# Gated linear attention, spectral mixing and a gated MLP on one core: the attention state kept compact, y in two PSUM banks, and a new order of the work

## The chip, the cores and the metric

The program runs on one NeuronCore of a Trainium2 chip. The metric is the device time of one launch in microseconds. Times of whole runs are medians over a few launches; everything about single instructions comes from one profiled execution of the kernel before. PE is TensorE (its weight loads are PEld), DVE VectorE, ACT ScalarE, POOL GpSimd, SP the engine that issues the transfers.

## The reference, cut

Three stages follow each other, on batch 4, sequence 768, 8 heads of 48 columns (384 channels):

```python
# 1. attention: a state of 48 x 48 for each head, decayed by alpha for each row
for t in range(S):
    state = alpha[:, :, t, :, None] * state + einsum('bhd,bhe->bhde', k[:, :, t], v[:, :, t])
    y[:, :, t] = einsum('bhd,bhde->bhe', q[:, :, t], state)
x = y as (batch, seq, 384)
# 2. spectral mixing
theta = x @ w_theta
zr, zi = x * cos(theta), x * sin(theta)
u = x + w_tok_r @ zr + w_tok_i @ zi          # 768 x 768 over the tokens
x = u + relu(u @ w_ch)
# 3. gated MLP
h = relu(x @ w_in)                           # 384 -> 1024
out = (h * sigmoid(conv3(h, conv_w))) @ w_out
```

Tokens are cut into 24 chunks of 128 (6 for each batch). Inside a chunk the attention is a product of scores with v; from chunk to chunk the state carries the rest.

## The kernel before

**Attention, per chunk.** VectorE runs two scans over alpha (L346, L360) and multiplies q and k by them (L375). TensorE makes the transposed k, `kps` (L395), and the scores `sc` (L398 to L405): eight products whose contraction is the 48 rows of one head; the even heads of the pairs lie on partitions 0 to 47, the odd ones on 64 to 111, and the two kinds go to two PSUM tiles in turn. ScalarE copies the scores out (`pt`, L410), GpSimd cuts the causal triangle (L411). Then `a_y` (L425) writes `y`, one PSUM tile of 128 x 384: 32 products `y<-v_t,pt` of 48 columns, each for 32 output rows, and, from a batch's second chunk on, 16 products `y<-S,qk_t`. For these the state S is 128 x 4 x 96: a pair of heads is a block of 96 columns, of which each head uses its own 48, the others are zero. `a_kv` (L448) makes the chunk's addition to the state: for chunks 0 to 11 (`FINEK`) in 8 products of 64 rows and 96 columns, after that in 16 products of 32 rows and 48 columns. `a_state` (L461) adds it to S (one sum of 112 x 384 at L477, or, from chunk 12 on, two of 48 x 192 at L475; a plain copy L472 in a batch's first chunk) and multiplies by the chunk's decay on GpSimd (L479, two instructions). ScalarE copies y to `x` (L446), TensorE transposes it (`xps`, L492), ScalarE copies that to `u` (L497).

**Mixing.** `th` is x @ w_theta, then `zf` goes ScalarE, VectorE, ScalarE (two sines), VectorE (L546, then L561) and is split in a high and a low part (L570 on ScalarE, `zl` L582 on VectorE). `m_mix` (L591) adds one chunk's share to `yps`: for three column blocks d and real and imaginary part, three products (high by high, high by low, low by high), so 18 for a half of the output tokens. For the chunks in `PLAINS` of batch 0 (0 and 1) z is kept in one piece, `zh<-x,zf`, and each of the 6 products is a full fp32 one, with w_tok in one piece too. `m_out_of` (L615) adds `yps` to u, once for each batch and half; for batch 2's second half that is called the sum (2,1) below. Weights arrive in 64-bit words that VectorE decodes in three steps (L169 to L171) before the split (L122 on ScalarE, L123 on VectorE).

**What sets the order.** The attention and `th` of batches 0 to 2, the mix of batches 0 and 1 and the scores of chunk 18 follow `ORDER`, a written list of steps; `in_order` (L652) holds each engine's instructions to that order. After it, the rest of batch 3's attention (chunks 18 to 23), the mix of batches 2 and 3, the decoding of w_ch, w_in and w_out and the MLP are placed by the framework's scheduler. Five PSUM banks (`ps_a`) are shared by y, kv, sc, kps, xps and th, three by yps. In this kernel the four quarters of w_in are loaded and decoded while batch 2's second half is mixed, through one staging buffer that is free when the attention's buffers are closed.

Of the kernel before, what the change touches and what calls it, by code (L numbers as in the profile page):

```python
# [43 lines left out]
PLAINS = (0, 1)  # L44
BYDMA = ()
ZBYDMA = ()
FINEY = 0
FINEK = 2 * NC
EARLY = 99
ORDER = (  # L50
# [44 lines left out]
def tile_gated_linear_attention__then__spectral_moe__then__conv_gate(  # L95
# [53 lines left out]
    def body(top, slow):  # L149
# [919 lines left out]
```

## Time and profile before

| what | us |
|---|---|
| median of 3 runs (lowest, highest) | 556.52 (554.0, 557.42) |
| the profiled execution | 554.66 |
| its span on the core | 552.9 |
| PE busy | 539.0 (97%) |
| DVE busy | 445.3 (81%) |
| ACT busy | 327.7 (59%) |
| POOL busy | 141.2 (26%) |

The profiled execution has 1.8 us around its span. TensorE's granted clock is 1.0 throughout. A matmul's duration in the rows includes its way through the array and overlaps the next one; what it costs in a stream is the distance from its start to the next start. An fp32 product stands as two records in the trace, an fp32r one as one.

### The profile page before, as it was taken

How to read it: one execution, taken by the hardware profiler on the slowest of the kernel's cores; microseconds unless marked ns; L12 is line 12 of the kernel's file. 1: busy time of each engine (PE TensorE's matmuls, PEld its weight loads, DVE VectorE, ACT ScalarE, POOL GpSimd, SP SyncE). 2: the span in 40 equal slices, each digit the busy share in tenths (PEclk: the TensorE clock that was granted, in tenths of full speed). 3: DMA queues.
4: the chain of work that ended last, by engine and by line, in shares of the span. 5: the costliest groups of instructions: out<-in, count | busy, mean ns of one | idle time of the engine just before them, and what ended most of it. 6: DMA issues, size and time to landing. Idle time of an engine off the chain costs nothing.

```text
span 552.9 us, 13205 instructions
## 1 busy us (share of the span) xinstructions
PE 539.0 (97%) x5421; PEld 473.9 (86%) x5423; DVE 445.3 (81%) x697; ACT 327.7 (59%) x699; POOL 141.2 (26%) x195
## 2 busy tenths in 40 slices
PE   7889999999999999999999999999999999999996
PEld 4567788688999999989998988898998898999896
DVE  7999999988975876753978789998989969969520
ACT  3657865656647683553743238757678567558621
POOL 2557644602122303450000002122224002314000
PEclk9999999999999999999999999999999999999999
DMA  8663664761132231401143351043253651500011
GB/s 327 190 236 102 227 204 133 241 191 48 30 116 79 88 112 36 134 29 58 59 140 116 117 187 42 0 145 127 86 188 129 219 181 55 205 28 16 30 45 47
DMA packets 24997, 65.56 MB, mean 119 GB/s; under 512 B 2529, under 2 KB 8673, under 8 KB 24545
## 3 DMA queue, kind: packets, MB, share of 16 engines
q1 hardware_dynamic: 24928, 64.64, 35.7%
q8 instruction: 44, 0.72, 0.5%
q14 instruction: 25, 0.20, 0.1%
HBM read 59.92 MB, written 4.72 MB: 117 GB/s over the span
## 4 chain that ended last, share of the span: by engine, by line
PE 85%; DVE 6%; DMA 5%; POOL 1%; issue 1%; ACT 0%; DVEq 0%; ACTq 0%; SPq 0%; POOLq 0%
PE yps L114 23%; PE ops L114 18%; PE hps L114 18%; PE cps L114 7%; PE th L114 6%; PE y L114 5%; PE sc L114 4%; DMA stage<-in_w_in_dram 3%; PE kv L114 2%; PE xps L492 1%; PE kps L395 1%; DVE fbt L346 1%; DMA stage<-in_w_tok_dram 1%; POOL S L479 1%; DVE stage L170 1%
## 5 line engine op out<-in xcount | busy, mean ns | idle before, releaser
L114 PE MATMUL yps<-wtok,zh 128*128 128x384 f32 x528 | 139.0, 343 | 1.1 <-DVE u L618 1.1
L114 PE MATMUL ops<-wout,g 128*128 128x384 f32 x576 | 104.4, 336 | 0.0
L114 PE MATMUL hps<-us,win 128*128 128x512 f32 x432 | 103.5, 390 | 0.0
L114 PEld LDWEIGHTS ops<-wout,g 128*128 128x128 f32 x576 | 101.0, 188 | 1.7
L114 PEld LDWEIGHTS yps<-wtok,zh 128*128 128x128 f32 x528 | 93.8, 188 | 4.7 <-DVE u L618 1.4
L114 PEld LDWEIGHTS hps<-us,win 128*128 128x128 f32 x432 | 80.8, 188 | 15.7
L114 PE MATMUL yps<-wtok,zl 128*128 128x384 f32 x264 | 87.4, 335 | 0.0
L842 DVE SCALAR_TENSOR_TENSOR cv<-hh,cw,cv 128x510 f32<-128x510 f32 (+7 forms) x128 | 74.7, 617 | 5.0 <-ACT cv L835 4.7
L411 POOL TENSOR_SCALAR_AFFINE_SELECT pt<-pt 128x512 f32<-128x512 f32 x48 | 51.5, 1087 | 99.1 <-ACT pt L410 95.5
L114 PEld LDWEIGHTS yps<-wtok,zl 128*128 128x128 f32 x264 | 49.5, 188 | 0.1
L123 DVE TENSOR_TENSOR g<-cv,g 128x384 fp32r<-128x384 f32 (+2 forms) x96 | 37.1, 423 | 10.3 <-ACT g L122 10.2
L479 POOL TENSOR_TENSOR S<-tst,ftot 48x192 f32<-48x192 f32 x32 | 34.2, 1068 | 39.1 <-DVE tst L475 19.0
L825 ACT ACTIVATE hh<-hps 128x512 f32<-128x512 f32 x48 | 28.5, 595 | 21.6 <-PE hps L114 12.5
L114 PE MATMUL cps<-us,wch 128*128 128x512 f32 x162 | 40.2, 390 | 0.0
L346 DVE TENSOR_TENSOR_SCAN fbt<-a_t,onehot 128x516 f32<-128x516 f32 x24 | 31.4, 1307 | 10.9 <-ACT a_t L367 9.1
L122 ACT CAST g<-cv 128x1 fp32r<-128x1 f32 (+3 forms) x128 | 37.2, 350 | 4.6 <-DVE cv L860 4.0
L860 DVE SCALAR_TENSOR_TENSOR cv<-cv,hh 128x511 f32<-128x511 f32 (+2 forms) x48 | 32.6, 691 | 7.1 <-ACT cv L859 7.1
L883 ACT ACTIVATE ob<-ops 128x384 f32<-128x384 f32 x24 | 11.7, 490 | 42.1 <-PE ops L114 42.1
L114 PEld LDWEIGHTS cps<-us,wch 128*128 128x128 f32 x162 | 30.4, 188 | 6.0
L835 ACT ACTIVATE cv<-hh,cw 128x511 f32<-128x511 f32 (+2 forms) x48 | 34.4, 724 | 1.4 <-POOL hh L828 0.7
L410 ACT COPY pt<-sc 128x512 f32<-128x512 f32 x48 | 26.7, 588 | 14.2 <-PE sc L114 10.2
L832 POOL COPY edge<-hh 128x2 f32<-128x2 f32 x32 | 14.3, 451 | 81.1 <-ACT hh L825 70.0
(101 smaller groups left out, 880.5 us busy)
## 6 DMA issues: line engine op xcount, KB each, us to landing
qk_t<-in_qka_dram SPq DMA_DIRECT2D x24, 512.0 KB, 4.9
stage<-in_w_tok_dram SPq DMA_DIRECT2D x12, 768.0 KB, 4.9
top<-in_w_tok_dram SPq DMA_DIRECT2D x12, 768.0 KB, 4.5
a_t<-in_qka_dram SPq DMA_DIRECT2D x24, 260.0 KB, 3.0
v_t<-in_v_dram SPq DMA_DIRECT2D x24, 192.0 KB, 4.1
out_dram<-ob SPq DMA_DIRECT2D x24, 192.0 KB, 1.9
stage<-in_w_in_dram SPq DMA_DIRECT2D x4, 768.0 KB, 4.4
stage<-in_w_out_dram SPq DMA_DIRECT2D x4, 768.0 KB, 4.4
```

The costliest lines, as they stand in the source:

```text
L114: nc.tensor.matmul(o, lhsT, rhs, start=start, stop=stop, skip_group_check=True)
L122: cast = nc.scalar.copy(hi, src)
L123: lo_eng.tensor_tensor(lo, src, hi.bitcast(F32), ALU.subtract)
L346: nc.vector.tensor_tensor_scan(bf[:, AW:0:-1], at[:, AW:0:-1], of[:, AW:0:-1], 0.0, ALU.mult, ALU.add)
L410: marks["pt"] = nc.scalar.copy(pt, scs[j])
L411: nc.gpsimd.affine_select(pt, pt, [[0, NP], [1, P]], ALU.is_ge, 0.0, base=0, channel_multiplier=-1)
L479: nc.gpsimd.tensor_tensor(Sn[r, :, e], tt[r, :, e], nft[r].unsqueeze(2).to_broadcast([D, NP, D]), ALU.mult)
L825: nc.scalar.activation(hh[:, 2:], ps, AF.Relu)
L832: nc.gpsimd.tensor_copy(edges[n][:, f], hh[:, CH : CH + 2])
L835: nc.scalar.activation(cv[:, a:e], hh[:, a + 1 : e + 1], AF.Copy, scale=cw[:, f, 1:2])
L842: nc.vector.scalar_tensor_tensor(cv[:, lo:hi], hh[:, lo + k : hi + k], cw[:, f, k : k + 1], cv[:, lo:hi], ALU.mult, ALU.add)
L860: nc.vector.scalar_tensor_tensor(cv[:, a:e], cv[:, a:e], 1.0, hhs.pop((n, f))[:, a + 1 : e + 1], ALU.add, ALU.mult)
```

## The change

The state S becomes 128 x 4 x 48: each head's own columns only. Its product `y<-S,qk_t` contracts over the 48 partitions of one head and writes 64 rows and 48 columns. The two heads of a pair lie on different partitions, so y is now two PSUM tiles, one for the even heads, one for the odd ones, each half of a bank wide; the first one's other half holds the chunk's addition `kv`, always in products of 32 rows and 48 columns. x is copied out in two instructions. The state's sum and its decay are one instruction each in every chunk, on 112 partitions x 192. `PLAINS` gets a third chunk. The loads of w_in move behind those of w_ch, after the scheduled loop, and the first decode step of each load that is issued there is ordered behind the sum (2,1). `ORDER` is a new list. The list's `warm` products, which only keep TensorE running at the start, are 36 in place of 39.

```diff
-PLAINS = (0, 1)
+PLAINS = (0, 1, 2)
...
-    "... kt.0 pt0.0 pt1.0 sq.1 tot.1 warm.9 y.0 kv.0 st.0 mul.1 "
+    "... fore.1 pt0.0 tot.1 pt1.0 kt.0 sq.1 mul.1 warm.9 kps.1 sc.1 y.0 kv.0 "
...
-            Sst = [acon.tile([P, NP, 2 * D], F32, name=f"S{i}") for i in range(2)]
+            Sst = [acon.tile([P, NP, D], F32, name=f"S{i}") for i in range(2)]
...
-                y = ps_a.tile([P, DM], F32, tag="a", name="y")
+                ybs = [ps_a.tile([P, 2, NP, D], F32, tag="a", name="y") for _ in range(2)]
+                y = [yb[:, 0] for yb in ybs]
+                if c < NC - 1:
+                    kvs[ci] = ybs[0][:, 1]
...
-                        for t in parts:
-                            mm(y[t, p * 96 : p * 96 + 96], qh[:, p, t], Sp[:, p, :], False, True)
+                        for t in (slice(0, 64), slice(64, P)):
+                            for j in range(2):
+                                r = slice(64 * j, 64 * j + D)
+                                mm(y[j][t, p], qh[r, p, t], Sp[r, p, :], False, True)
...
-                marks["x"] = nc.scalar.copy(xs[ci], ys.pop(ci))
+                xv = xs[ci].rearrange("p (a j d) -> p a j d", a=NP, j=2)
+                for j, yj in enumerate(ys.pop(ci)):
+                    marks["x"] = nc.scalar.copy(xv[:, :, j], yj)
...
-                        for i in range(0, P, rows):
-                            o = 2 * p * D + (i // 64 * D if fine else 0)
-                            mm(kv[i : i + rows, p, :], kt[:, p, i : i + rows], vt[:, o : o + wide], p == 0, True)
+                        for i in range(0, P, 32):
+                            o = 2 * p * D + i // 64 * D
+                            mm(kvs[ci][i : i + 32, p], kt[:, p, i : i + 32], vt[:, o : o + D], False, True)
...
-                        for r, e in own:
-                            nc.scalar.copy(Sn[r, :, e], kv[r, :, slice(0, D) if fine else e])
-                    elif fine:
-                        for r, e in own:
-                            nc.vector.tensor_tensor(tt[r, :, e], Sp[r, :, e], kv[r], ALU.add)
+                        nc.scalar.copy(Sn[:112], kv[:112])
                     else:
                         nc.vector.tensor_tensor(tt[:112], Sp[:112], kv[:112], ALU.add)
-                    for r, e in own:
-                        nc.gpsimd.tensor_tensor(
-                            Sn[r, :, e], tt[r, :, e], nft[r].unsqueeze(2).to_broadcast([D, NP, D]), ALU.mult
-                        )
+                    nc.gpsimd.tensor_tensor(
+                        Sn[:112], tt[:112], nft[:112].unsqueeze(2).to_broadcast([112, NP, D]), ALU.mult
+                    )
...
+            for k, ins in enumerate(decoding(full, st, n)):
+                if k == 0 and not slow:
+                    behind(ins, ("sum",))
...
+            marks["sum"] = sums[B - 2, 1]
...
+            for i in range(len(WIN_EARLY), 4):
+                load_in(i)
```

How this moves instructions, at three places. Names: `y<-S_113` and `y<-S_114` are the state's products (two buffers in turn), `y<-v_t,kt` after the change is the product that was `kv<-v_t,kt`, L114, L395, L492 are L113, L396, L488 afterwards.

TensorE near 36 us, from the `th` of chunks 1 and 2 to the scores of chunk 5, before:

```order
L114 MATMUL th<-whole,u 128x384 x6
L114 MATMUL yps<-full,zh 128x384 x2
L114 MATMUL y<-v_t,pt 32x48 x32
L114 MATMUL y<-S_114,qk_t 32x96 x16
L114 MATMUL kv<-v_t,kt 64x96 x8
L114 MATMUL yps<-full,zh 128x384 x2
L395 MATMUL kps<-ident,qk_t 128x128 x4
L492 MATMUL xps<-ident,x 128x128 x3
L114 MATMUL sc<-qk_t 128x128 x16
```

and after the change, from the `th` of chunk 2 to the scores of chunk 5:

```order
L113 MATMUL th<-whole,u 128x384 x3
L113 MATMUL yps<-full,zh 128x384 x4
L113 MATMUL y<-v_t,pt 32x48 x32
L113 MATMUL y<-S_114,qk_t 64x48 x16
L113 MATMUL y<-v_t,kt 32x48 x16
L396 MATMUL kps<-ident,qk_t 128x128 x4
L113 MATMUL sc<-qk_t 128x128 x8
L488 MATMUL xps<-ident,x 128x128 x3
L113 MATMUL yps<-full,zh 128x384 x4
L113 MATMUL sc<-qk_t 128x128 x8
```

Four units of plain mix (two products of `yps<-full` each) stand ahead of chunk 5's scores where there were two.

TensorE in the scheduled loop, around the scores of chunk 20, before:

```order
L492 MATMUL xps<-ident,x 128x128 x3
L395 MATMUL kps<-ident,qk_t 128x128 x4
L114 MATMUL sc<-qk_t 128x128 x8
L114 MATMUL y<-v_t,pt 32x48 x32
L114 MATMUL y<-S_114,qk_t 32x96 x16
L114 MATMUL kv<-v_t,kt 32x48 x16
```

and after the change, the same chunk:

```order
L113 MATMUL y<-v_t,kt 32x48 x16
L488 MATMUL xps<-ident,x 128x128 x3
L396 MATMUL kps<-ident,qk_t 128x128 x4
L113 MATMUL sc<-qk_t 128x128 x4
L113 MATMUL yps<-wtok,zh 128x384 x2
L113 MATMUL yps<-wtok,zl 128x384
L113 MATMUL yps<-wtok,zh 128x384 x2
L113 MATMUL yps<-wtok,zl 128x384
L113 MATMUL yps<-wtok,zh 128x384 x2
L113 MATMUL yps<-wtok,zl 128x384
L113 MATMUL yps<-wtok,zh 128x384 x2
L113 MATMUL sc<-qk_t 128x128 x4
```

The scores come as four of the even heads, mix products, and four of the odd heads (so for chunks 20, 21 and 22), and the state's addition no longer follows the state's product but stands after 13 to 21 mix products. Of the mix, 216 products (all of batch 2's) stand before batch 3's `th`, where there were 179; all six `th` (54 products) now follow each other.

VectorE behind the attention, before; `win` is the low part of a quarter of w_in, L517 the low part of x for `th`:

```order
L169 TENSOR_SCALAR stage<-stage 128x768
L170 SCALAR_TENSOR_TENSOR stage<-stage 128x768
L517 TENSOR_TENSOR zh<-u,zh 128x384
L171 SCALAR_TENSOR_TENSOR stage<-stage 128x768
L546 SCALAR_TENSOR_TENSOR zf<-zf,th 128x384
L123 TENSOR_TENSOR win_3639<-stage,win_3638 128x3x256
L546 SCALAR_TENSOR_TENSOR zf<-zf,th 128x384
L561 TENSOR_TENSOR zf<-x,zf 128x768 x2
L582 TENSOR_TENSOR zl<-zf,zh 128x768
```

and after the change (L614 is the sum (2,1), L168 to L170 the three decode steps, L513 the low part of x, L542, L557, L578 the three steps to `zl`):

```order
L614 TENSOR_TENSOR u<-yps,u 128x384 x3
L168 TENSOR_SCALAR stage<-stage 128x768
L169 SCALAR_TENSOR_TENSOR stage<-stage 128x768
L513 TENSOR_TENSOR zh<-u,zh 128x384
L170 SCALAR_TENSOR_TENSOR stage<-stage 128x768
L542 SCALAR_TENSOR_TENSOR zf<-zf,th 128x384 x2
L557 TENSOR_TENSOR zf<-x,zf 128x768 x2
L578 TENSOR_TENSOR zl<-zf,zh 128x768 x2
L542 SCALAR_TENSOR_TENSOR zf<-zf,th 128x384
L122 TENSOR_TENSOR wch_3955<-stage,wch_3954 128x768
```

The first weights decoded there are w_ch's, behind the sum (2,1); w_in's four quarters follow later, two of them ahead of the sums of batch 3's first half.

## Rows read from the trace of the kernel before

**Rows 1.** The page: busy time of TensorE.
```profile
PE 539.0 (97%) x5421; PEld 473.9 (86%) x5423; DVE 445.3 (81%) x697; ACT 327.7 (59%) x699; POOL 141.2 (26%) x195
```

**Rows 2.** The page: the chain that ended last, shares by engine.
```profile
PE 85%; DVE 6%; DMA 5%; POOL 1%; issue 1%; ACT 0%; DVEq 0%; ACTq 0%; SPq 0%; POOLq 0%
```

**Rows 3.** Two stretches: busy us of PE, PEld, DVE, ACT, POOL; clock, DMA.
```profile
50.00:100.00 50.00, 49.77 (x794) 39.53 (x786) 48.67 (x58) 35.60 (x74) 26.94 (x21) 1.00 0.60 188
...
350.00:400.00 50.00, 50.00 (x248) 44.67 (x247) 48.02 (x98) 34.28 (x81) 13.29 (x28) 1.00 0.28 93
```

**Rows 4.** TensorE's waits: for whom, us in total, times, longest.
```profile
PE yps L114 <- DVE u L618: 1.1, 1, 1.1
PE kv L114 <- issue: 1.1, 1, 1.1
PE y L114 <- POOL pt L411: 0.7, 2, 0.5
```

**Rows 5.** TensorE in order of time at 93 us (start, us, operation): an early chunk.
```profile
93.85 0.84 PE L114 MATMUL y<-S,qk_t 128*32 128x96 f32 x32
94.62 0.88 PE L114 MATMUL kv<-v_t,kt 128*64 128x96 f32 x16
95.44 0.66 PE L395 MATMUL kps<-ident,qk_t 128*128 128x128 f32 x4
96.02 1.16 PE L114 MATMUL sc<-qk_t 48*128 48x128 f32 x16
97.11 1.24 PE L114 MATMUL yps<-full,zh 128*128 128x384 f32 x3
```

**Rows 6.** The same at 223 us: a late chunk.
```profile
223.99 0.84 PE L114 MATMUL y<-S,qk_t 128*32 128x96 f32 x32
224.65 0.52 PE L114 MATMUL kv<-v_t,kt 128*32 128x48 f32 x32
225.10 0.44 PE L114 MATMUL yps<-wtok,zh 128*128 128x384 f32 x1
225.38 0.34 PE L114 MATMUL yps<-wtok,zl 128*128 128x384 f32 x1
```

**Rows 7.** The same at 100 us: plain mix, up to the next product.
```profile
100.77 2.74 PE L114 MATMUL yps<-full,zh 128*128 128x384 f32 x8
103.45 0.89 PE L114 MATMUL y<-v_t,pt 128*32 128x48 f32 x64
```

**Rows 8.** The chain that ended last, in order of time: start, us, what.
```profile
43.77 1.99 PE sc L114 x32
...
203.65 11.30 PE yps L114 x64
...
252.45 5.25 DMA stage<-in_w_in_dram
...
262.73 4.35 DMA stage<-in_w_in_dram
...
318.51 5.44 PE hps L114 x24
```

**Rows 9.** Groups of instructions by shape: count, busy us, mean ns; idle before.
```profile
L582 DVE TENSOR_TENSOR zl<-zf,zh 128x768 fp32r<-128x768 f32 x22 | 21.3, 972 | 2.6 <-ACT zh L570 2.5
L561 DVE TENSOR_TENSOR zf<-x,zf 128x768 f32<-128x768 f32 x22 | 21.1, 963 | 2.9 <-ACT zf L555 2.9
...
L475 DVE TENSOR_TENSOR tst<-S,kv 48x192 f32<-48x192 f32 x16 | 5.6, 350 | 8.7 <-PE kv L114 8.4
...
L477 DVE TENSOR_TENSOR tst<-S,kv 112x384 f32<-112x384 f32 x8 | 4.3, 541 | 0.6 <-PE kv L114 0.6
```

**Rows 10.** VectorE in order of time: product of chunk 5, then z of chunk 1.
```profile
42.63 1.22 DVE L375 TENSOR_TENSOR qk_t<-qk_t,fbt 128x1024 f32<-128x1024 f32 x1
...
45.82 1.26 DVE L561 TENSOR_TENSOR zh<-x,zf 128x768 f32<-128x768 f32 x1
```

**Rows 11.** GpSimd in order of time: one chunk's decay.
```profile
52.87 4.70 POOL L479 TENSOR_TENSOR S<-tst,ftot 48x192 f32<-48x192 f32 x2 [1.36 <-DVE tst L477]
```

More of the change, by code (lines that the diff above doesn't have):

```diff
@@ L38 @@
 NWARM = 13
+WIN_EARLY = ()
 OB = 2
@@ L43 @@
 WHOLE = 2
-PLAINS = (0, 1)
+PLAINS = (0, 1, 2)
 BYDMA = ()
 ZBYDMA = ()
-FINEY = 0
-FINEK = 2 * NC
 EARLY = 99
 ORDER = (
[36 rows of a table removed]
[36 rows of a table added]
 )
@@ L180, in load_split @@
             full = st[:, 1536 : 1536 + n]
-            decode(full, st, n)
+            for k, ins in enumerate(decoding(full, st, n)):
+                if k == 0 and not slow:
+                    behind(ins, ("sum",))
             if scale is not None:
@@ L429, in a_y @@
                 Sp = Sst[ci % 2]
-                y = ps_a.tile([P, DM], F32, tag="a", name="y")
-                rows = 32 if ci >= FINEY else 64
-                parts = [slice(i, i + rows) for i in range(0, P, rows)]
+                ybs = [ps_a.tile([P, 2, NP, D], F32, tag="a", name="y") for _ in range(2)]
+                y = [yb[:, 0] for yb in ybs]
+                if c < NC - 1:
+                    kvs[ci] = ybs[0][:, 1]
                 for j in range(2):
@@ L435, in a_y @@
                         h = 2 * p + j
-                        for t in parts:
-                            mm(y[t, h * D : (h + 1) * D], pts[j][:, p, t], vt[:, h * D : (h + 1) * D], h == 0, c == 0)
+                        for i in range(0, P, 32):
+                            t = slice(i, i + 32)
+                            mm(y[j][t, p], pts[j][:, p, t], vt[:, h * D : (h + 1) * D], p == 0, c == 0)
                 if c > 0:
                     for p in range(NP):
-                        for t in parts:
-                            mm(y[t, p * 96 : p * 96 + 96], qh[:, p, t], Sp[:, p, :], False, True)
+                        for t in (slice(0, 64), slice(64, P)):
+                            for j in range(2):
+                                r = slice(64 * j, 64 * j + D)
+                                mm(y[j][t, p], qh[r, p, t], Sp[r, p, :], False, True)
                 ys[ci] = y
@@ L451, in a_kv @@
                 if ci % NC < NC - 1:
-                    fine = ci >= FINEK
-                    rows, wide = (32, D) if fine else (64, 2 * D)
-                    kv = ps_a.tile([P, NP, wide], F32, tag="a", name="kv")
                     for p in range(NP):
-                        for i in range(0, P, rows):
-                            o = 2 * p * D + (i // 64 * D if fine else 0)
-                            mm(kv[i : i + rows, p, :], kt[:, p, i : i + rows], vt[:, o : o + wide], p == 0, True)
-                    kvs[ci] = kv
+                        for i in range(0, P, 32):
+                            o = 2 * p * D + i // 64 * D
+                            mm(kvs[ci][i : i + 32, p], kt[:, p, i : i + 32], vt[:, o : o + D], False, True)
             def a_state(ci):
@@ L466, in a_state @@
                     nft = prep[ci + 1][2] if ci + 1 in prep else half[ci + 1][4]
-                    fine = ci >= FINEK
-                    own = [(slice(64 * j, 64 * j + D), slice(j * D, (j + 1) * D)) for j in range(2)]
-                    tt = Sn if c == 0 else att.tile([P, NP, 2 * D], F32, tag="tst", name="tst", bufs=1)
+                    tt = Sn if c == 0 else att.tile([P, NP, D], F32, tag="tst", name="tst", bufs=1)
                     if c == 0:
-                        for r, e in own:
-                            nc.scalar.copy(Sn[r, :, e], kv[r, :, slice(0, D) if fine else e])
-                    elif fine:
-                        for r, e in own:
-                            nc.vector.tensor_tensor(tt[r, :, e], Sp[r, :, e], kv[r], ALU.add)
+                        nc.scalar.copy(Sn[:112], kv[:112])
                     else:
                         nc.vector.tensor_tensor(tt[:112], Sp[:112], kv[:112], ALU.add)
-                    for r, e in own:
-                        nc.gpsimd.tensor_tensor(
-                            Sn[r, :, e], tt[r, :, e], nft[r].unsqueeze(2).to_broadcast([D, NP, D]), ALU.mult
-                        )
+                    nc.gpsimd.tensor_tensor(
+                        Sn[:112], tt[:112], nft[:112].unsqueeze(2).to_broadcast([112, NP, D]), ALU.mult
+                    )
             def a_xt(ci):
@@ L587, in a_theta @@
                     f(ci)
-            mixps = {}
+            mixps, sums = {}, {}
             def m_mix(b, h, c, ds=range(KD)):
@@ L617, in m_out_of @@
                 for d in ds:
-                    nc.vector.tensor_tensor(ub[b][:, d, hs], mixps[d][:, :HALF], ub[b][:, d, hs], ALU.add)
+                    sums[b, h] = nc.vector.tensor_tensor(ub[b][:, d, hs], mixps[d][:, :HALF], ub[b][:, d, hs], ALU.add)
             def a_att(b, c):
@@ L712, in body, with load_in @@
                     win = [win_p.tile([P, KD, DFF], F32R, name=f"win{i}") for i in range(2)]
+                    def load_in(i):
+                        ns = slice(i * 256, (i + 1) * 256)
+                        wi = w_in.rearrange("(k p) f -> p k f", p=P).bitcast(U32)[:, :, 512 * i : 512 * (i + 1)]
+                        load_split(None, "w", wi, [KD, 256], win[0][:, :, ns], win[1][:, :, ns])
                 for c in range(NC):
@@ L715, in body @@
                     a_theta((b + 1) * NC + c)
-                    if b == B - 2 and c < 4:
-                        ns = slice(c * 256, (c + 1) * 256)
-                        wi = w_in.rearrange("(k p) f -> p k f", p=P).bitcast(U32)[:, :, 512 * c : 512 * (c + 1)]
-                        load_split(None, "w", wi, [KD, 256], win[0][:, :, ns], win[1][:, :, ns])
+                    if b == B - 2 and c in WIN_EARLY:
+                        load_in(WIN_EARLY.index(c))
             in_order(first, last)
```

72 rows, old and new, of the table ORDER are left out of this document.

## The prediction

> **What bounds the kernel now.** I read the page first: TensorE is busy for 539.0 of 552.9 us [rows 1], and 85% of the chain that ended last is TensorE's own work [rows 2]. Next its waits: the three that this change can touch come to 2.9 us [rows 4]. So a change pays here by the work that it takes from TensorE or by the order in which that work is fed, and what it spares the other engines pays nothing by itself. Then the stretches: from 50 to 100 us VectorE is busy for 48.67 of 50 us beside a full TensorE, and again for 48.02 from 350 to 400 [rows 3]. There a step of VectorE that comes late has little room to be made good. Last, TensorE in order of time, for what each product costs.
>
> **The change part by part.** The sum is made against the profiled execution, 554.66 us, which lies 1.9 below the median of the runs, 556.52; what comes out is put on the median.
>
> *The state's addition (kv).* By the starts, the old form costs 95.44 - 94.62 = 0.82 us [rows 5], the fine form 225.10 - 224.65 = 0.45 [rows 6]. Ten chunks (0 to 4 and 6 to 10) change from one to the other: -0.37 x 10 = **-3.7**.
>
> *The state's product.* Before, it costs 0.77 us where the old kv follows [rows 5] and 0.66 where the fine one does [rows 6]; what differs is the shape of the tile that comes next, so a change of shape costs about 0.11. The new product has the record count of the fine kv and its 48 columns, spread over two row and two column halves of the array. I take kv's 0.45 plus one change of shape in and some more for the two row halves: 0.65. That is -0.1 in 8 chunks and nothing in the other 12: **-0.8**. Nothing in the trace has this shape; below, it could cost 0.45 (-5.1 in all: 8 x 0.32 + 12 x 0.21); above, if the two row halves don't run side by side, 1.1 (+7.9: 8 x 0.33 + 12 x 0.44). The scores, which also use two row halves, take 1.09 us for 16 records [rows 5], and I take the value near the rows.
>
> The Trainium skill has a rule that speaks against this part: in "TensorEngine Tiling (Array Packing)", section "Key Properties", it says that "Changing tiling mode (not just tile) drains the TensorE". The 0.77 against 0.66 agrees with it. By the rule the new product adds such a drain in each of 20 chunks, and the sum is the one made here; without it, the lower bound of the product would hold.
>
> *A third plain chunk.* Plain mix costs (103.45 - 100.77) / 8 = 0.335 us a record [rows 7], split mix 11.30 / 64 = 0.177 [rows 8]. Chunk 2 of batch 0 has 36 split products, now 12 plain ones of two records: 24 x 0.335 - 36 x 0.177 = **+1.6**. It spares VectorE one `zl` (0.97) and ScalarE one cast.
>
> *The start.* Before, chunk 5's scores are over at 45.8 us [rows 8], with two units of plain mix behind TensorE. After, the order has four units ahead of them, so 2 x 4 x 0.335 = 2.7 us more work. What feeds them is VectorE's product for chunk 5, at 43.85 us [rows 10]. In the new order it stands behind one z more (1.26) and two first decode steps less (about 1.1), and three sums are smaller, 0.35 in place of 0.54 [rows 9]: 43.5. The scores (1.0 for 16 records, half of rows 8's first) then end at 44.7. So TensorE is 45.8 - 44.7 + 2.7 = 3.8 us ahead, of which chunks 0 to 3 had 1.8 by the two parts above: **-1.9**, with 1.5 either way for what I can't follow of ScalarE.
>
> *Smaller state steps.* The decay is one instruction in place of two; near 53 us the pair took 4.70 us [rows 11], and y waited for the triangle behind it, 0.7 in two waits [rows 4]: **-0.5**. The other sums and decays become shorter in the shadow of TensorE, as the mix products cover them. The second copy of x puts some 0.15 us a chunk on ScalarE, which is idle for 40% of the span; if a transpose did wait for each, that would be 3.6.
>
> *The scheduled loop.* Three chunks have their scores split. In one batch of eight, records run two at a time, 1.09 us; in a half nothing runs beside, so eight records take the pairs' time again plus the change of shape, 1.1 us for each half: +1.1 x 3 = **+3.3** (between 0 and 4). The state's addition alone between mix products has its own way in and out, some 0.1 each (225.38 - 225.10 = 0.28 for a first mix product that costs 0.177 in a stream [rows 6, 8]): 5 x 0.2 = **+1.0**.
>
> *Behind the attention.* Here the change adds a wait: VectorE's first decode step is ordered behind the sum (2,1) and waits for w_ch, and behind it in the queue stand the six chunks' `zf` and `zl`, for which batch 3's mix waits. Count from the start of the first transfer, at 252.45 before [rows 8]. It takes 5.25 us. Then VectorE has, up to `zl` of the fifth chunk, 6 `zf` of 0.5, 6 of 0.92 and 5 `zl` of 0.93 by their distances (means 0.963 and 0.972 [rows 9]), 0.5 for x, two decodes of 2.5 and two low parts of 0.95: 20.5. The second transfer (4.35 [rows 8]) starts when the first buffer has been read and has only some 3.3 us of this beside it, so 1.1 is waited, and ScalarE's sines hold VectorE for another 1 or 2: some 28.5 us. TensorE comes to that chunk after 19 mix products, a transpose, 54 `th` and 72 mix products: 145 x 0.175 + 0.3 = 25.7. So it waits for 2.8, and 0.2 at the first chunk: +3.0. The waits before in this stretch, 1.1 for the sum and 1.1 at a kv [rows 4], go: -2.2. Together **+0.8**, between -2 and +5. The last two quarters of w_in are decoded beside the second half's mix, over before the first `hps` (at 318.51 before [rows 8]).
>
> Sum: -3.7 - 0.8 + 1.6 - 1.9 - 0.5 + 3.3 + 1.0 + 0.8 = -0.2. On the median: **556.3 us**. The list gains some 5 us up to chunk 18, and the scheduled part gives them back.
>
> **The rivals.**
>
> *Faster: a change of the array's shape costs nothing beyond the records.* For it: `y<-v_t,pt` has four tiles at a time with no loss; against it: the 0.11 above. Then the state's product is at its lower bound (-4.3 on the sum), kv alone costs nothing (-1.0), and the six half scores lose their 0.2 (-1.2): 556.3 - 6.5 = **549.8**.
>
> *Slower: VectorE runs late into the MLP.* The four decodes of w_in, 3.4 us each, stood before 293 us, where VectorE had idle time. Two of them (6.9) now come later, and what they push, w_out's decodes, reaches the stretch from 350 us, where 2.0 of 50 us are free [rows 3]: 4.9 us that TensorE would wait for taps, and the wait behind the attention at 4 instead of 3. 556.3 + 5.9 = **562.2**. It decides from the point where TensorE's `hps` products stop following each other without a gap. Against it: between the sums of the first half and the first `hps` TensorE has 25 us of its own, and VectorE needs about 20 there.
>
> *Slower: the two row halves of the state's product run one after the other:* +8.7 over my term, **565.0**. The scores speak against it.
>
> **How the numbers follow.** The forecast has 0.64, the first rival 0.17, the second 0.13, the third 0.06. A measurement of this kernel can tell about 1%, 5.6 us, from no change. Faster by more: two thirds of the first rival and the end of the forecast's own spread, 0.17; slower by more: half of the second, the third, and the spread, 0.16; within 1%: 0.67. The range takes in -5.1 of the product's bounds beside the start's -1.5, and on the other side the +5 behind the attention and most of the second rival: 550.0 to 562.0.
>
> **What would show it.** In the profile after: kv at 0.45 us in an early chunk and the state's product at 0.6 to 0.7; chunk 5's scores over near 44.7 us with four plain units behind them; the loop's first 64 mix products beginning near 198.5 instead of 203.65; half scores of 1.1 us in three chunks; TensorE waiting some 3 us in all for `zl` behind the six `th`; and `hps` beginning at about the same time as before. It is wrong if the state's product costs under 0.5 or over 0.9, if `hps` begins more than 4 us away from 318.4, or if TensorE has gaps behind it.

## The result: 1.3% slower

| what | before | after |
|---|---|---|
| median of the runs, us (lowest, highest) | 555.60 (554.0, 557.42) | 562.96 (561.74, 564.21) |
| the profiled execution, its span | 554.66, 552.9 | 563.82, 562.1 |

The kernel before has one more run here than in the table of the start, hence 555.60 for 556.52. The ratio of the runs on record is 1.0126, 95% interval 1.0103 to 1.0150 (the quotient of the two medians is 1.0133). I had forecast 556.3, no change.

The page of the kernel after: busy time, and the chain that ended last by engine.

```profile
PE 544.7 (97%) x5567; PEld 473.1 (84%) x5568; DVE 437.7 (78%) x688; ACT 329.2 (59%) x718; POOL 109.0 (19%) x175
...
PE 90%; DVE 2%; DMA 2%; ACT 1%; issue 1%; ACTq 0%; DVEq 0%; SPq 0%
```

Against [rows 1], GpSimd and VectorE do less (141.2 to 109.0, 445.3 to 437.7), and that pays nothing: TensorE is still nearly all of the chain, 90% for the 85% of [rows 2], and it is busy for 5.7 us more. TensorE's waits after the change (for whom, us in total, times, longest):

```profile
PE xps L488 <- ACT x L453: 3.4, 2, 2.9
...
PE yps L113 <- DVE u L614: 2.2, 1, 2.2
PE yps L113 <- ACT zh L566: 1.2, 1, 1.2
...
PE y L113 <- ACT x L453: 0.8, 1, 0.8
```

The first and the last line are new beside [rows 4]: TensorE waits for x, ScalarE's copy of y. Four points of the program cut the difference to pieces (`hps` are the products with w_in, `cps` those with w_ch, `ops` those with w_out). They are read from TensorE's starts in order of time (some 0.1 us ahead of the chain's of [rows 8]); the forecast is that of the prediction.

| point, us | before | forecast | after | miss in the piece up to it |
|---|---|---|---|---|
| chunk 5's scores are over | 45.7 | 44.7 | 49.8 | +5.1 |
| the scheduled loop's mix begins | 203.6 | 198.5 | 205.8 | +2.2 |
| the first `hps` | 318.4 | 318.4 | 326.5 | +0.8 |
| end of the span | 552.9 | 552.7 | 562.1 | +1.3 |

Of the last +1.3, 1.1 lies behind TensorE's last product: from there to the end of the span it takes 5.8 us after the change and 4.7 before. That tail is between 4.7 and 6.4 us in all the runs below, and no edit aims at it. Most of the miss lies in the first 50 us. TensorE there, in order of time:

```profile
17.96 0.89 PE L113 MATMUL y<-v_t,pt 128*32 128x48 f32 x64
18.78 0.68 PE L113 MATMUL y<-S,qk_t 48*64 48x48 f32 x32
19.39 0.55 PE L113 MATMUL y<-v_t,kt 128*32 128x48 f32 x32
19.87 0.55 PE L488 MATMUL xps<-ident,x 128*128 128x128 f32 x3
23.32 0.55 PE L488 MATMUL xps<-ident,x 128*128 128x128 f32 x3 [2.90 <-ACT x L453]
23.70 0.63 PE L396 MATMUL kps<-ident,qk_t 128*128 128x128 f32 x4
24.26 2.08 PE L113 MATMUL sc<-qk_t 48*128 48x128 f32 x16
26.27 6.45 PE L113 MATMUL th<-whole,u 128*128 128x384 f32 x12
```

y and kv of chunk 1 are over at 19.87, yet its transposes start at 23.32, 2.90 us after TensorE could. ScalarE, which has to copy x for them:

```profile
19.20 0.52 ACT L453 COPY x<-y 128x192 f32<-128x192 f32 x2
22.73 0.54 ACT L453 COPY x<-y 128x192 f32<-128x192 f32 x2 [3.00 <-DVE tst L474]
```

It copies chunk 0's x, then sits idle for 3.00 us until VectorE has made the state's sum `tst` of chunk 1, and VectorE has two scans ahead of that:

```profile
21.21 1.23 DVE L361 TENSOR_TENSOR_SCAN fbt<-a_t,starts 128x516 f32<-128x516 f32 x1
22.36 0.33 DVE L474 TENSOR_TENSOR tst<-S,y 112x192 f32<-112x192 f32 x1
```

x does not need the sum. But kv now lies in the bank of half of y, so x and the sum read one bank, and the program puts the two engines' reads of it one behind the other; in the list, the sum of chunk 1 stands ahead of its x. The groups of x over the whole run, first of the kernel after, then of the one before (busy us, mean ns | idle before, and what ended it):

```profile
L453 ACT COPY x<-y 128x192 f32<-128x192 f32 x48 | 13.2, 328 | 19.4 <-DVE tst L474 11.3 <-PE y L113 8.0
```

```profile
L446 ACT COPY x<-y 128x384 f32<-128x384 f32 x24 | 11.5, 481 | 11.4 <-PE y L114 11.3
```

11.3 us of waiting for VectorE's sum is new. Then TensorE's clock. Three stretches after the change, and the same three before (length, busy us of PE, PEld, DVE, ACT, POOL, granted clock, DMA share, GB/s):

```profile
20.00:24.00 4.00, 1.10 (x9) 0.86 (x10) 3.90 (x7) 1.27 (x5) 0.75 (x1) 1.00 0.95 360
24.00:28.00 4.00, 4.00 (x22) 2.98 (x21) 2.87 (x4) 2.65 (x6) 0.91 (x2) 0.52 1.02 328
28.00:32.00 4.00, 4.00 (x9) 2.09 (x9) 0.87 (x2) 1.34 (x3) 0.31 (x1) 0.63 0.16 59
```

```profile
20.00:24.00 4.00, 2.76 (x42) 2.38 (x40) 3.64 (x7) 1.66 (x5) 0.12 (x1) 1.00 0.32 31
24.00:28.00 4.00, 3.40 (x14) 1.56 (x12) 3.87 (x5) 3.63 (x8) 3.85 (x3) 1.00 0.98 366
28.00:32.00 4.00, 2.69 (x116) 2.41 (x116) 4.00 (x5) 1.15 (x3) 1.70 (x2) 1.00 0.93 313
```

After the change TensorE works for 1.10 of 4 us, and then its granted clock is 0.52: nearly all of that stretch at the lower of its two levels, 1.2 GHz. The 16 score records take 2.01 us there (24.26 to 26.27) in place of 1.09 [rows 5], and twelve `th` 6.38 (26.27 to 32.65).

In the scheduled loop the forecast held. Chunk 20 and the neighbours of its scores:

```profile
223.12 0.55 PE L113 MATMUL y<-v_t,kt 128*32 128x48 f32 x32
...
224.51 1.16 PE L113 MATMUL sc<-qk_t 48*128 48x128 f32 x8
225.60 0.62 PE L113 MATMUL yps<-wtok,zh 128*128 128x384 f32 x2
...
227.73 1.16 PE L113 MATMUL sc<-qk_t 48*128 48x128 f32 x8
228.82 0.89 PE L113 MATMUL y<-v_t,pt 128*32 128x48 f32 x64
229.64 0.68 PE L113 MATMUL y<-S,qk_t 48*64 48x48 f32 x32
230.25 0.44 PE L113 MATMUL yps<-wtok,zl 128*128 128x384 f32 x1
```

Each half of the scores costs 1.09 us, as much as the whole did, and kv stands alone (a lone kv below: mix products on both sides).

### The profile page after: what moved, and what is told of

The parts are those of the page before. It is cut to its first block, busy times and chain, and to the rows that moved or that the text cites. A ratio compares the mean times of both kernels' runs of the same rounds, so it can differ in the third digit from the quotient of the medians.

```text
span 562.1 us, 13445 instructions
## 1 busy us (share of the span) xinstructions
PE 544.7 (97%) x5567; PEld 473.1 (84%) x5568; DVE 437.7 (78%) x688; ACT 329.2 (59%) x718; POOL 109.0 (19%) x175
## 4 chain that ended last, share of the span: by engine, by line
PE 90%; DVE 2%; DMA 2%; ACT 1%; issue 1%; ACTq 0%; DVEq 0%; SPq 0%
PE yps L113 25%; PE ops L113 18%; PE hps L113 17%; PE th L113 8%; PE y L113 7%; PE cps L113 7%; PE sc L113 5%; PE xps L488 2%; PE kps L396 1%; DMA stage<-in_w_in_dram 1%; DMA stage<-in_w_ch_dram 1%; DVE zl L578 0%; DVE stage L169 0%; DVE fbt L347 0%; ACT x L453 0%
## 5 line engine op out<-in xcount | busy, mean ns | idle before, releaser
L113 PE MATMUL yps<-wtok,zh 128*128 128x384 f32 x504 | 130.6, 343 | 3.5 <-DVE u L614 2.2
L113 PE MATMUL ops<-wout,g 128*128 128x384 f32 x576 | 104.1, 336 | 0.0
L113 PE MATMUL hps<-us,win 128*128 128x512 f32 x432 | 103.6, 390 | 0.0
L113 PEld LDWEIGHTS ops<-wout,g 128*128 128x128 f32 x576 | 101.0, 188 | 1.6
L113 PEld LDWEIGHTS yps<-wtok,zh 128*128 128x128 f32 x504 | 89.4, 188 | 7.0 <-DVE u L614 2.5
L113 PEld LDWEIGHTS hps<-us,win 128*128 128x128 f32 x432 | 80.8, 188 | 15.9
L113 PE MATMUL yps<-wtok,zl 128*128 128x384 f32 x252 | 83.0, 337 | 0.0
L845 DVE SCALAR_TENSOR_TENSOR cv<-hh,cw,cv 128x255 f32<-128x255 f32 (+7 forms) x128 | 75.2, 616 | 4.7 <-ACT cv L838 4.4
L412 POOL TENSOR_SCALAR_AFFINE_SELECT pt<-pt 128x512 f32<-128x512 f32 x48 | 41.9, 885 | 122.8 <-ACT pt L411 122.7
L113 PEld LDWEIGHTS yps<-wtok,zl 128*128 128x128 f32 x252 | 47.1, 188 | 0.5 <-DVE zl L578 0.3
L113 PE MATMUL cps<-us,wch 128*128 128x512 f32 x162 | 40.7, 390 | 0.0
L862 ACT ACTIVATE cv<-cv 128x511 f32<-128x511 f32 (+2 forms) x48 | 29.9, 628 | 9.9 <-DVE cv L845 9.6
L113 PEld LDWEIGHTS cps<-us,wch 128*128 128x128 f32 x162 | 30.3, 188 | 5.9
L113 PE MATMUL sc<-qk_t 48*128 48x128 f32 x384 | 32.3, 291 | 0.0
L113 PEld LDWEIGHTS sc<-qk_t 48*128 48x128 f32 x384 | 27.0, 193 | 5.3 <-issue 3.2
```

Source lines behind the costliest of these rows:

```text
L113: nc.tensor.matmul(o, lhsT, rhs, start=start, stop=stop, skip_group_check=True)
L412: nc.gpsimd.affine_select(pt, pt, [[0, NP], [1, P]], ALU.is_ge, 0.0, base=0, channel_multiplier=-1)
L845: nc.vector.scalar_tensor_tensor(cv[:, lo:hi], hh[:, lo + k : hi + k], cw[:, f, k : k + 1], cv[:, lo:hi], ALU.mult, ALU.add)
L862: nc.scalar.activation(cv[:, a:e], cv[:, a:e], AF.Tanh, scale=0.5)
```

## The experiments

My theory from this trace: kv in y's bank (a part to which the prediction gave no price) makes x late; TensorE idles, its clock falls; the rest is what shape changes, lone kv and half scores cost. Rivals: the late loads of w_in; the new list with its third plain chunk; a clock that costs nothing because TensorE would wait anyway. Fifteen runs, each with its ratio to the kernel before and the 95% interval; the points are those of the table above, from one profiled execution each. Those of early and oldorder were the fastest of their four runs, 1.3 and 3.1 us below the median. In early, oldorder and oldkv 16 to 18 more `cps` products, about 4 us, stand ahead of the first `hps`, so that point and the pieces that end there can't be set beside the others' as they are.

| kernel | median us | ratio | chunk 5's scores over | loop's mix | first `hps` | end of span |
|---|---|---|---|---|---|---|
| after | 562.96 | 1.0126 (1.0103 to 1.0150) | 49.8 | 205.8 | 326.5 | 562.1 |
| warm | 560.72 | 1.0088 (1.0055 to 1.0121) | 46.6 | 201.5 | 323.8 | 558.6 |
| x1 | 560.43 | 1.0071 (1.0047 to 1.0096) | 45.0 | 200.5 | 319.8 | 557.3 |
| ownbank | 556.89 | 1.0002 (0.9986 to 1.0018) | 45.1 | 202.0 | 316.8 | 555.0 |
| early | 564.25 | 1.0163 (1.0126 to 1.0200) | 48.3 | 203.8 | 330.2 | 561.2 |
| oldorder | 563.86 | 1.0151 (1.0113 to 1.0189) | 46.7 | 203.2 | 328.0 | 559.1 |
| kvmid | 554.31 | 0.9957 (0.9934 to 0.9980) | 49.7 | 202.8 | 315.9 | 553.8 |
| kvlist | 562.13 | 1.0099 (1.0067 to 1.0130) | 49.0 | 202.3 | 322.0 | 560.8 |
| oldkv | 561.75 | 1.0097 (1.0064 to 1.0131) | 49.1 | 204.9 | 325.4 | 560.5 |
| kvwarm | 549.82 | 0.9869 (0.9842 to 0.9897) | 46.3 | 198.9 | 311.0 | 548.2 |
| kvx1 | 549.92 | 0.9891 (0.9864 to 0.9918) | 44.9 | 198.3 | 310.3 | 548.5 |
| xall | 550.11 | 0.9882 (0.9857 to 0.9908) | 46.7 | 199.6 | 311.7 | 548.4 |
| kvx1early | 556.49 | 0.9999 (0.9975 to 1.0023) | 45.0 | 198.3 | 318.9 | 555.3 |
| kvx1half | 555.92 | 0.9988 (0.9968 to 1.0007) | 45.0 | 198.4 | 319.7 | 554.6 |
| fine | 557.35 | 1.0022 (1.0001 to 1.0044) | 48.6 | 205.2 | 320.1 | 555.9 |
| finewarm | 555.51 | 0.9996 (0.9970 to 1.0021) | 49.6 | 206.4 | 319.3 | 554.2 |

**The start: warm, x1, ownbank.** The first leaves the wait and fills it with products whose result nobody uses:

```diff
-x.1 tot.3 xt.1 kps.2
+x.1 tot.3 warm.13 xt.1 kps.2
```

> Edit: 13 more warm products in the list ahead of the transposes of chunk 1, where TensorE waited 2.9 us for x; nothing else. Theory A (the idle time lets TensorE's clock fall, and the fall costs the time): granted clock 1.0 from 24 to 32 us, the first 12 th take 4.1 us in place of 6.4 and the scores before them 1.1 in place of 2.0, chunk 5's scores are over near 46.5 us in place of 49.8, and the time falls by 3.3 us, to about 559.7. Rival (TensorE would have waited for VectorE's decoding of w_theta there anyway, the clock costs nothing of its own): clock 1.0, but the waits grow, and the time falls by less than 1 us.

The same stretches:

```profile
20.00:24.00 4.00, 3.85 (x24) 2.10 (x22) 3.90 (x7) 1.19 (x5) 0.75 (x1) 1.00 0.91 342
24.00:28.00 4.00, 4.00 (x28) 2.75 (x27) 2.95 (x5) 2.98 (x7) 1.52 (x2) 1.00 1.00 329
```

TensorE is kept busy, the clock stays at 1.00 (over the whole span it is 0.989 to 0.994 in the four executions of the changed kernel and 0.995 to 0.997 in those of warm), and chunk 5's scores are over 3.2 us earlier, at 46.6 as forecast by theory A. The span of the profiled execution is 3.5 us shorter, the median falls by 2.2, and the two intervals overlap, so the size is not sharp. The rival is out for the trace: the clock has its own price at the start.

The second takes the wait away by order alone: x of chunk 1 ahead of its sum, on ScalarE and TensorE nothing moves.

```diff
-fore.3 st.1 wh.0 wh.0 mul.3 wo.0 x.1 tot.3
+fore.3 x.1 st.1 wh.0 wh.0 mul.3 wo.0 tot.3
```

> Edit: in the list the copy x of chunk 1 stands before that chunk's state sum instead of behind it; on ScalarE and TensorE nothing moves. Theory: x is copied near 19.9 us, the transposes end near 20.5 and the scores of chunk 2 near 22.5, then TensorE waits for w_theta until about 25: the wait is not removed but moved behind the scores, 1 us is won and the clock still falls: about 562. Rival (the wait for x alone is what the start lost): no wait ahead of the first th, clock 1.0, 559.5 or less.

```profile
20.60 0.55 PE L487 MATMUL xps<-ident,x 128*128 128x128 f32 x3 [0.18 <-ACT x L452]
20.98 0.60 PE L395 MATMUL kps<-ident,qk_t 128*128 128x128 f32 x4
21.51 0.48 PE L112 MATMUL sc<-qk_t 48*128 48x128 f32 x2
22.75 1.16 PE L112 MATMUL sc<-qk_t 48*128 48x128 f32 x14 [0.75 <-DVE tst L473]
23.84 4.14 PE L112 MATMUL th<-whole,u 128*128 128x384 f32 x12
```

My theory of this run fell, and the rival is right in the trace (its 559.5 us were 560.4): 2.90 us of waiting became 0.18 and 0.75 at the scores behind, `th` starts at 23.84 without the wait for w_theta that I expected, the clock is 1.0, and chunk 5's scores are over at 45.0, where the prediction had 44.7. One late copy of x was what the start's term lacked. Of the 4.7 us between the changed kernel and x1 up to there, 2.0 are waits of TensorE (4.1 against 2.1 us) and 2.8 are `th` and scores that cost less at the higher clock (8.42 to 6.11 and 7.47 to 7.03 us by the starts). (The 2.2 us ahead of the first product, the same in all, are left out.) The kernel before waits for 3.8 us up to there as well, but at a clock of 1.00. From the first `hps` on 1.9 us of it are lost again: `ops` now waits 2.7 us for ScalarE.

The third undoes the part itself: kv gets its own bank, as before; all else stays.

```diff
-                if c < NC - 1:
-                    kvs[ci] = ybs[0][:, 1]
...
+                    kvs[ci] = ps_a.tile([P, NP, D], F32, tag="a", name="kv")
...
```

> Edit: kv gets a PSUM tile of its own again, as before; y stays in two banks, the state compact, the list as after the change. Theory (two readers of one bank take turns: x waits for VectorE's sum of the same bank, and kv waits for x): TensorE's waits for x, 2.9, 0.5 and 0.8 us, go; at the start TensorE still waits for the decoding of w_theta, so of the first only about 1 us is won: 2 us in all, about 561. Rival (seven tiles a chunk on five banks): new waits of y or of the scores for a bank, the same time or more.

The time is the one before the change (1.0002), 6 us less than after it, three times what I expected. The group of x, whose wait for the sum is gone:

```profile
L451 ACT COPY x<-y 128x192 f32<-128x192 f32 x48 | 13.2, 328 | 9.6 <-PE y L113 9.6
```

Besides the start (45.1) the loop gains as well: from its mix to the first `hps` 114.8 us, as before the change, for 120.7 after it. There kv follows the state's product, and two of the three split chunks have whole scores again:

```profile
231.24 0.90 PE L113 MATMUL y<-v_t,pt 128*32 128x48 f32 x64
232.07 0.68 PE L113 MATMUL y<-S,qk_t 48*64 48x48 f32 x32
233.44 0.55 PE L113 MATMUL kv<-v_t,kt 128*32 128x48 f32 x32 [0.68 <-ACT pt L411]
...
236.62 1.17 PE L113 MATMUL sc<-qk_t 48*128 48x128 f32 x16
```

So the split scores and the lone kv, which the prediction priced well, come for the most part from the shared bank too, by way of the scheduler: kv has to write the bank before or after x reads it, and in chunk 19 above kv starts at 223.12, when x is over (by ScalarE's rows, at 220.80). kvmid below takes the lone kv and the split scores away and leaves the bank shared, so this part of the 6 us is a price of the place that kv was given, and not of every order with a shared bank. The rival's new waits exist (1.8 us of kv for `pt`, 1.2 for x), but are smaller.

**The list and the loads: oldorder, early.** early is the first line of this edit, oldorder all of it:

```diff
-WIN_EARLY = ()
+WIN_EARLY = (0, 1, 2, 3)
-PLAINS = (0, 1, 2)
+PLAINS = (0, 1)
...
-    "back.0 fore.0 tot.0 sq.0 mul.0 kps.0 sc.0 back.1 hl.0 load.2 load.3 load.4 wl.0 load.5 wl.1 load.6 load.7 "
+    "back.0 fore.0 mul.0 kps.0 sc.0 tot.0 sq.0 back.1 fore.1 hl.0 load.2 wl.0 load.3 wl.1 wl.2 load.4 load.5 "
...
```

(in oldorder the whole list is that of the kernel before).

> Edit: the compact state, y in two banks and kv in y's bank as after the change, but the list of steps, the two plain chunks and the early loads of w_in of the kernel before. Theory (the loss is the list's: its start, its third plain chunk): kv, state's product and y<-v_t,pt together -3.8 us, half scores +3.2, lone kv +0.5, clock 1.0 throughout: about 555.5, no change against the kernel before. Rival (kv in y's bank makes ScalarE's x and VectorE's sum wait for each other in any list): waits of TensorE for x, time 558 or more.

> Edit: all four quarters of w_in are loaded beside batch 2's second half again, as in the kernel before; the rest as after the change. Theory: the stretch behind the attention costs about what I predicted, so the time falls by about 1 us (the 2.2 and 1.2 us of waits there shrink, TensorE's waits at the loop's end come back): about 562. Rival (the late loads are what makes the changed kernel slow): 5 us or more, 558 or below, with hps beginning 5 us earlier against the loop's start.

oldorder is as slow as the changed kernel: the loss is there without the new list, the third plain chunk and the late loads, and my theory of this run is out. (It puts back all three at once, so what each of them is worth alone it does not say.) The rival has the time, and a wait of TensorE for x of 1.3 us; the clock falls at the start here too, to 0.63 from 28 to 32 us. From the loop's mix to the first `hps` it takes 124.8 us; 18 more `cps` products stand in that piece than before, at 2.04 us for nine 4.1 us, so 5.9 more than the 114.8 before, which is what the changed kernel loses there. early cannot be told from the changed kernel; the late loads are not what makes that one slow.

**Shape changes and split scores: kvmid, kvlist, oldkv.** kv's products have the tile shape of y's first kind (128 rows by 32 columns), the state's product has another. kvmid puts kv between the two, wherever its kt is copied before y; kvlist does so only for chunks below 18 (`if kts.get(ci) and ci < 18:`); oldkv is oldorder with kvmid's edit.

```diff
+                if kts.get(ci):
+                    kv_mm(ci)
+                    kvdone.add(ci)
                 if c > 0:
```

> Edit: where a chunk's kt is copied before its y in the list, the kv products stand between y's two kinds (they have the tile shape of the first kind); the rest as after the change. Theory (each change of the array's shape costs about 0.11 us, a kv alone between other products about 0.2): 11 lone kv and 5 pairs of shape changes go, -2.7; the six half scores of the scheduled loop become whole, -3.2: together -5.9, about 557.1. Rival (shape changes cost nothing, the rise of y<-v_t,pt from 0.70 to 0.82 us has another cause): -3.2 from the scores alone, 559.8. Second rival (TensorE now waits for the copy of kt): waits of TensorE for ScalarE's kt of 3 us or more, no gain.

> Edit: kv between y's two kinds only in the chunks of the written list (0 to 17); the five chunks of the scheduled loop keep kv behind y, and their scores stay split in three chunks. Theory (kvmid's 8.7 us are two things: shape changes in the list, whole scores and fewer waits in the loop): between chunk 5's scores and the loop 2.9 us as in kvmid, the loop to the first hps as after the change: about 560, 3 us less than the changed kernel. Rival (the list's part is nothing, all of it is the loop): 563.

> Edit: oldorder (compact state in the list, the two plain chunks and the early loads of the kernel before) with kv between y's two kinds. Theory (what made oldorder slow is shape changes, lone kv and split scores): scores -2.9, seven lone kv -1.4, ten pairs of shape changes -1.1, y's waits as they are: 5.5 less than oldorder, about 558.4. Rival (the old list waits for the banks that two tiles of y hold, whatever kv's place): less than 2 us gained, 562.

One chunk of kvmid:

```profile
32.73 0.89 PE L113 MATMUL y<-v_t,pt 128*32 128x48 f32 x64
33.43 0.52 PE L113 MATMUL y<-v_t,kt 128*32 128x48 f32 x32
33.88 0.68 PE L113 MATMUL y<-S,qk_t 48*64 48x48 f32 x32
34.49 0.66 PE L396 MATMUL kps<-ident,qk_t 128*128 128x128 f32 x4
```

y's first kind costs 0.70 us ahead of kv and 0.82 ahead of the state's product (17.96 to 18.78 above), kv 0.45 there and 0.48 ahead of the transposes. A change of shape is 0.12 us, near the 0.11 of the prediction, and the rival that it costs nothing is out. kvmid is 8.7 us faster than the changed kernel, 2.8 more than expected, and faster than the kernel before. From chunk 5's scores to the loop it takes 153.1 us for 156.0, and from the loop's mix to the first `hps` 113.1 for 120.7: by the starts, the scores there cost 5.46 for 8.69 (all are whole), and the mix products 4.4 less: 2.4 of that are waits (3.5 for the sum and `zh` became 1.1 for `zl`), 2.0 the products themselves, which are broken into less often. The second rival's wait for kt is not in the trace. From the first `hps` to the end kvmid loses 2.3 us of this (237.9 for 235.6). kvlist has the first gain (153.3) and not the second; its sum is not in the time, because in the MLP `ops` waits 2.3 us and the granted clock falls behind that (0.57 from 370 to 374 us). oldkv has its rival's time (561.75 for 562), but whether TensorE waits for y's banks, as the rival has it, the trace does not tell. Its scores are whole, while the start ends 2.4 us later, with 2.3 us in front of chunk 3's scores for which the profile names no releaser and a clock of 0.62 from 36 to 40, and TensorE waits 2.2 us for the low part of x behind the attention.

**Together: kvwarm, xall, kvx1.** kvwarm is kvmid's edit and warm's, kvx1 is kvmid's and x1's, and xall is kvwarm with x1's move for all eight chunks whose x stood behind their sum (0 to 4, 9, 13, 14).

> Edit: kv between y's two kinds (as in kvmid) and the 13 warm products ahead of chunk 1's transposes (as in warm). Theory (the two costs are independent): 554.3 - 2.2 = 552.1, with the clock at 1.0 from 20 to 32 us. Rival (what the start wins VectorE gives back, since it has 2 or 3 us free from 50 to 100 us): 554.

> Edit: kvmid, and chunk 1's x ahead of its state sum in the list as in x1, without the added warm products. Theory (x1 and warm take away the same loss at the start, once by the wait, once by the clock): 549.8 as kvwarm, clock 1.0. Rival (part of warm's gain is not that wait): 552.

> Edit: kvwarm, and in the list the x of each of the eight chunks whose state sum stood ahead of it moves before that sum. Theory (ScalarE's x waits for VectorE only in that order): ScalarE's waits for the sum go, TensorE's 0.5 us wait for x goes, 0.5 us less than kvwarm: 551.6. Rival (ScalarE's order gets worse, since x now stands ahead of copies that TensorE needs first): 1 us more, 553.

All three are near 550, some 13 us below the changed kernel and 1.1 to 1.3% below the kernel before; on top of kvmid the start is worth 4.4 us, more than I expected. warm and x1 are two cures for one loss: xall has both and gains no more. The other seven x give nothing that can be told. kvwarm is the best, 0.9869 (0.9842 to 0.9897).

**The loads once more: kvx1early, kvx1half.** kvlist and x1 lost time in the MLP, so I tried the loads of w_in once more, on kvx1:

```diff
-WIN_EARLY = ()
+WIN_EARLY = (0, 1, 2, 3)
```

and `(0, 1)` for kvx1half.

> Edit: kvx1, with all four quarters of w_in loaded beside batch 2's second half again. Theory (when the front is faster, the two late quarters push w_out's decoding into the stretch from 350 us, where VectorE is full, and some 2 us of the front's gain is lost there): from the first ops to the end 196 us in place of kvx1's 198.0, but TensorE waits 1 to 2 us more behind the attention as in early: 549 to 550. Rival (the loads' place doesn't matter, the order of the MLP is chance): from the first ops to the end 198 again, 550 to 551.

> Edit: kvx1, with two quarters of w_in loaded beside batch 2's second half and two behind it. Theory: as kvx1early, but with half of the waits behind the attention: 548.5. Rival: 550, no change.

My theories of both runs fell, and so did the rivals: four early quarters cost 6.6 us, two cost 6.0. The loss arises behind the attention (first `hps` at 318.9 for 310.3). TensorE waits there for batch 2's sum and for the parts of x that `th` needs, in kvx1early, and then in kvx1:

```profile
PE yps L112 <- DVE u L625: 2.8, 2, 2.6
PE th L112 <- ACT zh L515: 2.7, 1, 2.7
```

```profile
PE yps L112 <- DVE zl L589: 0.9, 1, 0.9
```

These waits are 4.6 us of the 8.6; in most of the rest, 3.9 us, the mix and `th` products cost more by the starts, since the clock falls behind the waits (0.93 on average from 250 to 300 us, for 1.00 in kvx1). From the first `hps` to the end kvx1early takes 236.4 us for 238.2, so the MLP gives 1.8 back, about what I expected; but ahead of it 8.6 are lost, where my theory had 1 to 2. Late loads are worth 6.6 us in a program that is fast up to there, and in the changed kernel nothing that can be told.

**One part alone: fine, finewarm.** The kernel before with kv in small products everywhere (fine), and that with eight more warm products (finewarm):

```diff
-FINEK = 2 * NC
+FINEK = 0
...
-warm.1 kps.3
+warm.9 kps.3
```

> Edit, to the kernel before: kv in products of 32 rows and 48 columns in all chunks (FINEK 0 in place of 12), which is the first part of the change by itself; state, y, list and loads stay as before. Theory (kv's 0.37 us in ten chunks and 0.11 us of a shape change in eight are TensorE time on the path): -4.6, about 552. Rival (VectorE, which gets two sums of 0.35 us in place of one of 0.54 where it is full, gives it back): 556.5, no change.

> Edit: fine (the kernel before with fine kv in all chunks), and eight more warm products ahead of chunk 3's transposed k, where TensorE idles about 2 us. Theory (fine's start was lost because a shorter kv leaves TensorE idle for longer and its clock falls): clock 1.0 from 32 to 40 us, the 12 th there 4.1 us in place of 5.5, 1.5 to 3 us less than fine, 554.5 to 556. Rival (the loss is the 1.7 us wait at chunk 3's scores alone, which the profile gives no releaser for): no gain, 557.

fine gains nothing (its rival's time; that VectorE is the reason the trace does not show). At the start TensorE waits more with the shorter kv, and the clock falls (0.79 from 32 to 40 us; `issue` marks a wait for which the profile shows no releaser):

```profile
32.18 0.71 PE L114 MATMUL sc<-qk_t 48*128 48x128 f32 x7
34.57 0.72 PE L114 MATMUL sc<-qk_t 48*128 48x128 f32 x9 [1.68 <-issue]
35.22 0.78 PE L492 MATMUL xps<-ident,x 128*128 128x128 f32 x3
35.78 5.54 PE L114 MATMUL th<-whole,u 128*128 128x384 f32 x12
```

In finewarm the wait in front of these scores is 2.53 us and the clock of that stretch 0.79 again, so the warm products did not do what they did in warm; its time can't be told from fine's. What TensorE waits for at these scores stays open.

## Why the prediction was wrong

- **kv in y's bank.** The failed step. The change's description has it, and no term of the sum did: I priced the second copy of x and did not ask who else reads its bank. ownbank shows what it costs in this order of the work, 6 us of the 7.4: at the start x waits for VectorE's sum (2.90 us of TensorE, and the clock behind it), in the loop kv is kept away from y. kvmid and x1 together win more than that back with the bank still shared; a bank of its own together with kvmid's order was not run. The Trainium skill has the rule: "PSUM — Partial Sum Buffer", section "PSUM bank collisions raise a hardware error", says that two engines must not touch one bank in the same quadrant of 32 partitions at a time, two readers included, so their accesses have to be put in order by bank. By the 11.3 us that x waited for VectorE the trace agrees that they are ordered; what happens without the order no run here shows.
- **The start, -1.9.** Came out at about +3.2 (-1.9 and the miss of 5.1). x1 puts the time right: with that one wait gone chunk 5's scores end at 45.0 for the forecast's 44.7. But that the two numbers are so near is partly luck. The forecast had VectorE's product, at 43.5, set this time; in x1 the product is over at 42.3, and TensorE comes to the scores at 43.95 straight from the four plain units, without a wait. I had written 1.5 us either way "for what I can't follow of ScalarE"; it was there, but of another size, since the clock fell behind the idle time. My reading of the waits was short as well: the three of [rows 4] leave out TensorE's two waits at the start of the kernel before, 1.2 us for VectorE's sum and 1.9 without a releaser, in the very piece where the loss arose. (43.5 and 1.0 make 44.5, not 44.7; that changes nothing.)
- **kv, -3.7, and the state's product, -0.8.** Over all chunks by the starts, without waits, kv fell by 3.2 (13.03 to 9.87) and the state's product by 2.4 (14.67 to 12.23), but y's first kind rose by 1.9, because the change of shape is paid in front of the new product. Together -3.7 for -4.5: the sizes were right (0.48 for 0.45, 0.61 for 0.65). In fine, kv's part bought nothing: the step from less TensorE work to less time fails where TensorE waits (there 1.7 us for VectorE's sum, and 2.2 and 1.7 without a releaser).
- **The third plain chunk, +1.6.** 24 records added 7.9 us (15.78 to 23.70), 0.33 each, as taken; right (the sum as written makes +1.7).
- **The scheduled loop, +3.3 and +1.0, and behind the attention, +0.8.** 120.7 us for the forecast 119.9: right in sum. The halves cost 1.09 for 1.1. TensorE's waits behind the attention, 3.4 us, were for the sum and `zh` where I expected `zl`.
- **From chunk 5 to the loop** 156.0 for the forecast 153.8: the 0.8 us wait of kv for x (the shared bank again), 0.9 with no releaser in the profile; and the transposes, to which I gave no term, cost 0.9 more (`kps` 5.55 for 5.15, `xps` 4.69 for 4.19 by the starts). The smaller state steps, -0.5, bring nothing to be seen: the two waits for the triangle went, one for x came.
- **The rivals.** VectorE late into the MLP is not in the changed kernel (from the first `ops` to the end 196.8 us for 195.8, the 1.0 being the tail behind TensorE's last product), but kvlist (200.0) and x1 (198.8) show a loss there once the front is faster, at waits for ScalarE's `hh` by the profile. Free shape changes and row halves one after the other are both out. The right time came near the second rival's, by another mechanism.

## What to carry to other kernels

Before two tensors share a PSUM bank, list who reads each: here the two readers were put one behind the other, and the later one inherited the earlier one's whole queue. A wait of TensorE costs more than its length when the clock falls behind it (4.7 us at chunk 5's scores for one wait of 2.90); with kv in its new place, filling it with idle products or reordering one instruction gave back the same time. Products of one tile shape belong next to each other (0.12 us for each change of shape here), and a gain of TensorE's work counts only from the point where TensorE is the one that is late.

## What was not expected of the hardware

After 1.10 us of work in 4 us TensorE ran at a granted clock of 0.52 for the next four, while before the change 2.76 of 4 was followed by 1.00. But the same wait need not have the same end. In kvx1early and in kvx1half, two executions with nearly the same work behind the attention, TensorE waits 2.7 and 2.6 us for the same part of x; in the first the clock falls there, in the second it does not, though TensorE did less in the four microseconds (kvx1early, then kvx1half; from 290 to 300 us it is 0.83 in both):

```profile
264.00:268.00 4.00, 2.06 (x6) 1.66 (x7) 4.00 (x7) 1.82 (x3) 0.00 (x0) 0.76 0.00 0
268.00:272.00 4.00, 4.00 (x20) 4.00 (x20) 3.98 (x7) 2.70 (x5) 0.00 (x0) 0.81 0.00 0
```

```profile
264.00:268.00 4.00, 1.07 (x5) 0.52 (x4) 3.90 (x6) 1.82 (x3) 0.00 (x0) 1.00 0.01 2
268.00:272.00 4.00, 4.00 (x24) 4.00 (x24) 4.00 (x8) 1.59 (x3) 0.00 (x0) 1.00 0.00 0
```

So the price of a wait that is read from one execution holds for that execution. And TensorE waited 1.7 to 2.5 us at chunk 3's scores in fine and finewarm without a releaser that the profile shows, beside a DMA share of 0.70 to 0.76 from 32 to 40 us.
